# Interleaving the high and low parts of W_out in a channel-attention and feed-forward kernel

## The chip, the cores and the metric

The kernel runs on one NeuronCore of one Trainium2 chip. The metric is the device time of one execution in microseconds (us). A profile of one execution, taken by the hardware profiler, comes with it.

## The reference

For each of four batches, 6080 tokens with 256 channels: q and k are normalised over the tokens, a 256 x 256 attention matrix over the channels is formed, and v is multiplied with it. A feed-forward layer with a leaky ReLU follows.

```python
def _attn_ref(q, k, v, tau):
    qn = q / (np.linalg.norm(q, axis=1, keepdims=True) + 1e-06)
    kn = k / (np.linalg.norm(k, axis=1, keepdims=True) + 1e-06)
    s = kn.transpose(0, 2, 1) @ qn / tau
    a = softmax(s, axis=-1)          # written out in the reference, with 1e-9 in the sum
    return (v @ a).astype(np.float32)

def _moe_ref(x, w_in, w_out):        # w_in 256 x 2048, w_out 2048 x 256, both float64
    h = x @ w_in
    g = np.maximum(0.01 * h, h)
    return (g @ w_out).astype(np.float32)
```

The inputs q, k and v are float32, the two weights are float64, and the result is float32.

## The kernel before, in words

**Number format.** A float32 value is held as two parts in the type float32r: the high part is the value cast to float32r, and the low part is what the cast left out. A product of two such values takes three matmuls: high x high, low x high, high x low. Nearly all products are made so. Only the scores of batch 0 and of the first groups of batch 1 are computed directly from float32 operands.

**Weights.** The float64 weights arrive as pairs of 32-bit words. `f64_load` brings a block of 512 columns into the tile f64_raw (f_raw in the profile), whose last dimension is the pair, and `f64_split` makes the high and low parts: VectorE and ScalarE instructions at lines 323 to 335 rebuild the float32 value, reading the low and high words with a step of two. Then line 338 (ScalarE cast) writes the high part and line 339 (VectorE subtract) the low part. There are 16 such blocks, 8 of W_in and 8 of W_out. `wo_block` gives the destination for W_out: slices of `wo[0]` (high) and `wo[1]` (low). Both are views of the tile `wo_hl` (w_out_split in the profile), which stays in SBUF for the whole kernel. The 8 blocks of W_out are converted in the first 172 us, between other work.

**Tiles.** The tokens are worked on in tiles of 2 x 512 columns, the last of a batch in 2 x 480. There are 6 tiles in each of 4 batches, and 8 pairs of feed-forward blocks in each tile: 192 iterations of the main loop.

**The main loop.** In each iteration `block_product` (line 551) computes the four quarters of the hidden layer with seven block products, three matmuls each. Its stationary operands are the tile w_split, its moving ones v_split. ScalarE and VectorE then take the sums out of PSUM, apply the leaky ReLU (line 562) and split the result into g_split (lines 563 and 565). `ffn_out` (line 597) multiplies g_split with W_out: for each of four quarters and two halves of the output channels three matmuls, so 24 for an iteration, 4608 in all. Their stationary operand is a 128 x 128 piece of `wo[x]`, their moving one a part of g_split with 512 or 480 columns, and they accumulate in four PSUM banks (ps_o).

**Order.** The order on TensorE is written out by hand. `ffn_out` is a generator, and `out(n)` draws its next n matmuls; they stand between the block products of the following iteration, in runs of 5, 5, 8 and the rest, where they fill the time in which ScalarE and VectorE work on the hidden layer. The queues `todo`, emptied by `slot`, put the work for the next batch (casts, scores at line 182, the new weights at line 401) into the gaps. DMAs are issued from the sync engine's queue.

**Each matmul has a weight load of its own**: TensorE loads the stationary operand (LDWEIGHTS, in the profile's row PEld) and then streams the moving operand past it (MATMUL, row PE). The load of one matmul is issued while the one before it is still streaming.

Of the kernel before, what the change touches and what calls it, by code (L numbers as in the profile page):

```python
# [10 lines left out]
F32R = mybir.dt.float32r  # L11
# [6 lines left out]
P = 128  # L18
# [13 lines left out]
def channel_attention_ffn(  # L32
# [18 lines left out]
    B, N, C = q.shape  # L51
    CH = C // P
    DFF = w_in.shape[1]
    NF = DFF // P
# [12 lines left out]
    const = ctx.enter_context(tc.tile_pool(name="const", bufs=1))  # L67
# [6 lines left out]
    def bank(tag, bufs=1):  # L74
        return psum.tile([P, TW], F32, name="ps_" + tag, tag=tag, bufs=bufs)
# [11 lines left out]
    rtau = const.tile([P, 1], F32, name="rtau")  # L87


    wo_hl = const.tile([P, 2 * NF * C + P], F32R, name="w_out_split")  # L90
    wo = [wo_hl[:, x:x + NF * C].rearrange("p (f d) -> p f d", d=C) for x in (0, NF * C + P)]
    zeros = const.tile([P, P], F32, name="zeros")
    nc.vector.memset(zeros, 0.0)

# [759 lines left out]
    for i in range(NTILES):  # L854
        for p in range(NPAIR):
# [6 lines left out]
            x, y, z = bank("x"), bank("y"), bank("z")  # L862
# [63 lines left out]
```

## Time and profile before

| what | value |
|---|---|
| time, median of 2 runs | 2225.53 us (2225.09 to 2225.98) |
| span of the profiled execution, first to last instruction | 2225.9 us |
| mean granted TensorE clock in it | 0.990 |
| TensorE matmuls | 2174.0 us busy, 9940 matmuls |
| weight loads | 1814.1 us busy, 9940 loads |
| VectorE / ScalarE | 1488.5 / 1483.2 us busy |
| matmuls of line 597 (W_out) | 3840 with 512 columns, 768 with 480 |

The profile gives, beside these, the span in 40 slices (busy tenths of each engine, and the clock granted to TensorE in tenths of full speed), the chain of work that ended last, groups of equal instructions with their mean duration, windows with the busy time of each engine, and a timeline. In a timeline row stand the start, the length, the engine, the line, the operation, the output and the inputs, the shape and the count of like instructions that follow one another; a bracket gives idle time ahead of them. Matmuls overlap on TensorE and their ends are modelled, so what a matmul costs is read from the distance between the starts of successive ones.

### The profile page before, as it was taken

Reading aid. Unit: us, or ns where it says so; the run is one execution under the profiler, and the core shown is the slowest. Engines: PE = TensorE matmul, PEld = TensorE weight load, DVE = VectorE, ACT = ScalarE, POOL = GpSimd, SP = SyncE. Lnnn points to the kernel's source line nnn. Section 1 sums busy time; section 2 is a strip of 40 time slices with the busy share of each in tenths; the row PEclk is TensorE's granted clock in tenths of the full one; section 3 lists DMA queues with packets and bytes.
Section 4 is the critical chain, followed back from the end, with each engine's and each line's share of the span. In section 5 each row is a group of like instructions: output and inputs, shape, how many; then the busy total and the mean of one; then the engine's idle time right before and its main releaser. Section 6 shows DMA issues by size and latency. Waiting matters only on the chain.

```text
span 2225.9 us, 27253 instructions
## 1 busy us (share of the span) xinstructions
PE 2174.0 (98%) x9940; PEld 1814.1 (81%) x9940; DVE 1488.5 (67%) x2651; ACT 1483.2 (67%) x2563; POOL 2.8 (0%) x10
## 2 busy tenths in 40 slices
PE   9679999999999999999999999999999999999999
PEld 7467888888888888888887888888888888888887
DVE  7986667666766776666766667676677655556554
ACT  6556777766657777776656777777665666666665
POOL 0000000000000000000000000000000000000000
PEclk9889999999999999999999999999999999999999
DMA  9435343342753434433464344343354432332331
GB/s 347 145 142 200 121 155 134 130 157 83 241 204 112 156 123 145 154 116 138 147 227 156 119 159 159 115 155 129 121 192 156 146 137 83 138 121 100 119 118 36
DMA packets 98967, 324.74 MB, mean 146 GB/s; under 512 B 10257, under 2 KB 22033, under 8 KB 98833
## 3 DMA queue, kind: packets, MB, share of 16 engines
q1 hardware_dynamic: 98832, 323.00, 42.1%
q8 instruction: 78, 1.28, 0.2%
q14 instruction: 57, 0.46, 0.1%
HBM read 264.50 MB, written 58.46 MB: 145 GB/s over the span
## 4 chain that ended last, share of the span: by engine, by line
PE 89%; DVE 5%; DMA 3%; ACT 2%; issue 0%; SPq 0%; ACTq 0%; DVEq 0%
PE ps_o L597 44%; PE ps_x L551 22%; PE ps_z L551 11%; PE ps_y L551 5%; PE ps_s L182 5%; PE ps_s L401 1%; DMA qk_raw<-in_k_dram 1%; DVE h L572 1%; DVE g_split L565 1%; DMA w_dram<-w_rest 1%; ACT h L562 1%; ACT g_split L563 1%; DMA f_raw<-in_w_out_dram 1%; DMA qk_raw<-in_q_dram 1%; DVE v_split L516 0%
## 5 line engine op out<-in xcount | busy, mean ns | idle before, releaser
L597 PE MATMUL ps_o<-g_split,w_out_split 128*128 128x512 f32 (+1 forms) x4608 | 1165.5, 388 | 0.0
L597 PEld LDWEIGHTS ps_o<-g_split,w_out_split 128*128 128x128 f32 x4608 | 867.7, 188 | 175.5
L565 DVE TENSOR_TENSOR g_split<-h,g_split 128x512 fp32r<-128x512 f32 (+1 forms) x768 | 525.0, 684 | 395.3 <-ACT g_split L563 394.4
L551 PE MATMUL ps_x<-v_split,w_split 128*128 128x512 f32 (+1 forms) x2304 | 653.7, 392 | 29.4 <-DVE w_split L439 16.2
L562 ACT ACTIVATE h<-h 128x512 f32<-128x512 f32 (+1 forms) x576 | 361.8, 628 | 292.3 <-DVE h L572 292.3
L578 ACT COPY h<-ps_x 128x512 f32<-128x512 f32 (+1 forms) x576 | 334.3, 580 | 312.4 <-PE ps_x L551 311.7
L551 PEld LDWEIGHTS ps_x<-v_split,w_split 128*128 128x128 f32 x2304 | 423.7, 189 | 114.0 <-ACT h L578 12.4
L563 ACT CAST g_split<-h 128x512 fp32r<-128x512 f32 (+1 forms) x768 | 473.4, 616 | 23.9
L572 DVE TENSOR_TENSOR h<-ps_z,h 128x512 f32<-128x512 f32 (+1 forms) x384 | 262.0, 682 | 284.7 <-ACT h L578 278.0
L551 PE MATMUL ps_z<-v_split,w_split 128*128 128x512 f32 (+1 forms) x1152 | 324.4, 390 | 6.3 <-DVE h L572 6.3
L551 PEld LDWEIGHTS ps_z<-v_split,w_split 128*128 128x128 f32 x1152 | 216.5, 188 | 52.5 <-DVE h L572 8.1
L551 PE MATMUL ps_y<-v_split,w_split 128*128 128x512 f32 (+1 forms) x576 | 162.9, 391 | 0.6 <-ACT w_a L411 0.6
L572 DVE TENSOR_TENSOR h<-ps_y,h 128x512 f32<-128x512 f32 (+1 forms) x192 | 131.3, 684 | 0.6
L551 PEld LDWEIGHTS ps_y<-v_split,w_split 128*128 128x128 f32 x576 | 109.0, 190 | 23.5 <-ACT w_a L411 1.1
L182 PEld LDWEIGHTS ps_s<-qk_split 128*128 128x128 f32 x804 | 114.1, 190 | 11.3 <-issue 1.0
L562 ACT ACTIVATE h<-ps_x 128x512 f32<-128x512 f32 (+1 forms) x192 | 112.8, 587 | 10.8 <-PE ps_x L551 10.8
L182 PE MATMUL ps_s<-qk_split 128*128 128x256 f32 x804 | 118.1, 283 | 0.0
L160 ACT CAST qk_split<-qk_raw 128x512 fp32r<-128x512 f32 x134 | 82.9, 619 | 31.8 <-PE ps_s L182 24.0
L516 DVE TENSOR_TENSOR v_split<-v_raw,v_split 128x512 fp32r<-128x512 f32 (+1 forms) x144 | 98.7, 686 | 4.7
L155 DVE TENSOR_TENSOR sq_acc<-sq_acc,sq 128x512 f32<-128x512 f32 x141 | 96.2, 683 | 0.0
L164 DVE TENSOR_TENSOR qk_split<-qk_raw,qk_split 128x512 fp32r<-128x512 f32 x134 | 91.6, 684 | 2.3 <-ACT qk_split L160 2.3
L152 ACT ACTIVATE sq<-qk_raw 128x512 f32<-128x512 f32 x141 | 88.8, 633 | 2.0 <-DMA qk_raw<-in_k_dram 2.0
(101 smaller groups left out, 726.7 us busy)
## 6 DMA issues: line engine op xcount, KB each, us to landing
w_split<-w_dram SPq DMA_DIRECT2D x184, 896.0 KB, 4.7
qk_raw<-in_q_dram SPq DMA_DIRECT2D x92, 256.0 KB, 3.6
qk_raw<-in_k_dram SPq DMA_DIRECT2D x92, 256.0 KB, 3.8
v_raw<-in_vT_dram SPq DMA_DIRECT2D x40, 512.0 KB, 4.9
out_dram<-o_sb SPq DMA_DIRECT2D x80, 256.0 KB, 4.2
win<-win_dram SPq DMA_DIRECT2D x24, 512.0 KB, 4.1
w_dram<-w_rest SPq DMA_DIRECT2D x24, 512.0 KB, 3.1
w_dram<-w_first SPq DMA_DIRECT2D x24, 384.0 KB, 3.4
```

What stands on the lines that cost most here:

```text
L152: return nc.scalar.activation(out=out, in_=self.chunk(j), func=AF.Square)
L155: return nc.vector.tensor_tensor(out=self.acc[0], in0=self.acc[0], in1=sq, op=ALU.add)
L164: return nc.vector.tensor_tensor(out=sp[:, :, 1, :], in0=self.chunk(j), in1=f32(sp[:, :, 0, :]), op=ALU.subtract)
L182: mm = nc.tensor.matmul(out=s, lhsT=lhsT, rhs=rhs, start=False, stop=last and n == len(passes) - 1, skip_group_check=True,)
L516: last = nc.vector.tensor_tensor(out=sp[:, 1, 0:w], in0=src, in1=f32(sp[:, 0, 0:w]), op=ALU.subtract)
L551: mm = nc.tensor.matmul(out=ps[:, 0:n], lhsT=w[:, x, a, :], rhs=sp[:, y, 0:n], start=first and k == 0, stop=k == 2, skip_group_check=True,)
L562: nc.scalar.activation(out=out[:, 0:n], in_=h[:, 0:n], func=AF.Prelu, alpha=0.01)
L563: issued["act"] = nc.scalar.copy(out=sp[:, 0, 0:n], in_=out[:, 0:n])
L565: issued["dve"] = nc.vector.tensor_tensor(out=sp[:, 1, 0:n], in0=out[:, 0:n], in1=f32(sp[:, 0, 0:n]), op=ALU.subtract)
L572: issued["dve"] = nc.vector.tensor_tensor(out=h[:, 0:n], in0=ps[:, 0:n], in1=h[:, 0:n], op=ALU.add)
L578: issued["act"] = nc.scalar.copy(out=h[:, 0:n], in_=ps[:, 0:n])
L597: issued["pe"] = nc.tensor.matmul(out=o_ps[i][j][h][:, 0:n], lhsT=wo[x][:, f, h * P:(h + 1) * P], rhs=sp[:, y, 0:n], start=p == 0 and earl ...
```

## The change

The tile w_out_split held the 4096 values of the high part of each partition, a gap of 128 values, and the 4096 of the low part. Now it holds pairs: the high and the low part of one value stand side by side, with 64 unused pairs at the end. The tile has 8320 values per partition in both kernels. Every view `wo[x]` now has a step of two values in its last dimension: `f64_split` writes it with that step, and the weight loads of line 597 read their 128 columns with it. Nothing else in the source is changed.

```diff
-    wo_hl = const.tile([P, 2 * NF * C + P], F32R, name="w_out_split")
-    wo = [wo_hl[:, x:x + NF * C].rearrange("p (f d) -> p f d", d=C) for x in (0, NF * C + P)]
+    wo_hl = const.tile([P, NF * C + P // 2, 2], F32R, name="w_out_split")
+    wo = [wo_hl[:, 0:NF * C, x].rearrange("p (f d) -> p f d", d=C) for x in range(2)]
```

## The prediction

> **What bounds the kernel now.** The reading goes from the page's busy shares and slices to its chain, and from there to the weight loads. The first fence holds the page's engine line, the slices of TensorE (PE) and of its granted clock, and the chain of work that ended last.
>
> ```profile
> PE 2174.0 (98%) x9940; PEld 1814.1 (81%) x9940; DVE 1488.5 (67%) x2651; ACT 1483.2 (67%) x2563; POOL 2.8 (0%) x10
> PE   9679999999999999999999999999999999999999
> PEclk9889999999999999999999999999999999999999
> PE 89%; DVE 5%; DMA 3%; ACT 2%; issue 0%; SPq 0%; ACTq 0%; DVEq 0%
> ```
>
> TensorE carries 89% of the chain, and after the third slice it neither rests nor loses clock. The next fence has two tables of windows (busy time and count of each engine, granted clock, DMA share, GB/s). The first two rows are of all instructions: a stretch at half clock, a steady one at full clock. The last two are of the instructions that touch w_out_split alone.
>
> ```profile
> 85.00:89.00 4.00, 3.32 (x9) 2.62 (x9) 2.84 (x8) 1.77 (x3) 0.00 (x0) 0.50 0.41 166
> 300.00:400.00 100.00, 100.00 (x482) 84.26 (x481) 68.60 (x111) 74.63 (x130) 0.00 (x0) 1.00 0.43 150
> ...
> 0.00:172.00 172.00, 28.99 (x106) 21.43 (x106) 5.48 (x8) 4.93 (x8) 0.89 0.59 211
> 172.00:2226.00 2054.00, 1136.56 (x4502) 846.24 (x4502) 0.00 (x0) 0.00 (x0) 1.00 0.41 140
> ```
>
> In 300 to 400 us TensorE is busy all the time, and the two vector engines have 31 and 25 us to spare. 4502 of the 4608 matmuls that use W_out lie behind 172 us, in such stretches. So the question is what paces one matmul after another. A matmul's own duration doesn't tell it, because matmuls overlap; the distance from start to start does. The rows below are of the timeline (start, length, engine, line, tile, count); the first is the fp32 score product of batch 0, the next three are at the half clock, the next four at full clock, and the last is the tail.
>
> ```profile
> 19.68 28.65 PE L182 MATMUL ps_o<-qk_raw 128*128 128x256 f32 x132
> ...
> 86.71 1.48 PE L551 MATMUL ps_z<-v_split,w_split 128*128 128x512 f32 x3
> 87.99 1.48 PE L551 MATMUL ps_x<-v_split,w_split 128*128 128x512 f32 x3
> 89.27 0.63 PE L401 MATMUL ps_y<-win_early,aT 128*128 128x512 f32 x1
> ...
> 1316.30 0.84 PE L551 MATMUL ps_y<-v_split,w_split 128*128 128x512 f32 x3
> 1316.98 1.30 PE L597 MATMUL ps_o<-g_split,w_out_split 128*128 128x512 f32 x5
> 1318.12 0.88 PE L182 MATMUL ps_s<-qk_split 128*128 128x256 f32 x6
> 1318.83 0.40 PE L551 MATMUL ps_x<-v_split,w_split 128*128 128x512 f32 x1
> ...
> 2214.89 6.66 PE L597 MATMUL ps_o<-g_split,w_out_split 128*128 128x480 f32 x30
> ```
>
> At half clock, three fp32r matmuls of 512 columns take 89.27 - 87.99 = 1.28 us, or 426.7 ns each. Halved, that is what 512 columns cost at full clock if nothing else costs: 213.3 ns, 0.417 ns a column. Measured at full clock: (1316.98 - 1316.30) / 3 = 226.7 ns, and five W_out matmuls take 1.14 us, 228 ns each, the same within the rounding. So each fp32r matmul of 512 columns pays 226.7 - 213.3 = 13.4 ns beyond its columns. In the tail 29 steps (6.66 us less the last matmul's own 0.38, from the group rows below) make 216.6 ns for 480 columns that should take 200.0: 16.6 ns beyond. In the fp32 row 131 steps take (28.65 - 0.39) / 131 = 215.7 ns for 256 columns. That is 0.84 ns a column, twice the fp32r one; against two times 256 column times, 213.3 ns, only 2.4 ns are beyond, though a weight load stands before each of those matmuls as well.
>
> The excess is therefore no fixed price of a load and a matmul. It appears where the moving operand is streamed at a column every 0.417 ns, and it all but vanishes where a column takes twice that. I read it as the load's reads of the buffer getting in the way of a stream that has no slack.
>
> The weight loads come next: groups by form (busy, mean ns), and two timeline rows for their pace.
>
> ```profile
> L597 PE MATMUL ps_o<-g_split,w_out_split 128*128 128x512 f32 x3840 | 977.3, 390 | 0.0
> L597 PEld LDWEIGHTS ps_o<-g_split,w_out_split 128*128 128x128 f32 x4608 | 867.7, 188 | 175.5
> L597 PE MATMUL ps_o<-g_split,w_out_split 128*128 128x480 f32 x768 | 188.2, 381 | 0.0
> L182 PE MATMUL ps_o<-qk_raw 128*128 128x256 f32 x192 | 42.8, 386 | 0.0
> L182 PEld LDWEIGHTS ps_s<-qk_raw 128*128 128x128 f32 x40 | 7.4, 190 | 3.9 <-DMA qk_raw<-in_k_dram 2.5 <-issue 0.5
> ...
> 52.87 1.08 PEld L200 LDWEIGHTS ps_y<-ones,sq_acc 128*128 128x128 f32 x8
> 53.87 0.30 PEld L182 LDWEIGHTS ps_s<-qk_raw 128*128 128x128 f32 x2
> ```
>
> A load's record of 188 ns is latency and reading together. Where eight loads follow one another with matmuls of a single column between, they take 53.87 - 52.87 = 1.00 us, at most 125 ns each. So a contiguous load of 128 elements holds its path for up to 125 ns, under a matmul of 213.3 ns: it has some 88 ns of cover. Loads of fp32 and fp32r show the same record (190 and 188 ns), so the two kinds of matmul differ in the stream, not in the load.
>
> **The change part by part.** The matmuls, their order, the DMAs and the queues stay as they are; no wait and no instruction is added. Two things change: how 16 instructions write W_out's parts, and how 4608 loads read them.
>
> The writes. In the conversions, the operand f_raw already holds pairs of words read with a step of two, so the trace prices steps on the vector engines:
>
> ```profile
> L323 DVE TENSOR_SCALAR f_scale<-f_raw 128x512 int32<-128x512 int32 x16 | 6.7, 422 | 1.0 <-DMA f_raw<-in_w_out_dram 1.0
> L515 DVE CAST v_split<-v_raw 128x512 fp32r<-128x512 f32 x120 | 50.1, 419 | 0.0
> L329 ACT ACTIVATE f_raw<-f_raw 128x512 f32<-128x512 uint32 x16 | 10.9, 681 | 13.5 <-DMA f_raw<-in_w_out_dram 10.3 <-DMA f_raw<-in_w_in_dram 3.1
> L338 ACT CAST w_out_split<-f_x 128x512 fp32r<-128x512 f32 x8 | 4.9, 618 | 6.9 <-DVE f_x L335 6.9
> L339 DVE TENSOR_TENSOR w_out_split<-f_x,w_out_split 128x512 fp32r<-128x512 f32 x8 | 5.5, 685 | 0.1
> ```
>
> VectorE reads with a step of two at 422 ns against 419 dense: nothing. ScalarE at line 329 reads and writes with the step, in place, at 681 ns; the dense cast at line 338 takes 618. Eight casts could thus grow by 8 x 63 ns = 0.5 us. A stepped write of VectorE is in no row; its bounds are nothing and a doubling, 8 x 685 ns = 5.5 us. I take 0.5 us for all, nearest to the rows. It falls before 172 us.
>
> The reads. No row shows a stationary operand with a step. Its price per matmul lies between two ends. Below: the whole excess goes, 3840 x 13.4 + 768 x 16.6 = 51.5 + 12.7 = 64 us gained. Above: the stepped load passes over 1024 bytes of a partition instead of 512, and if what it takes from the stream goes with that, the excess doubles: 64 us lost. The value in between depends on which row is the likeness. I take the fp32 row, by a conjecture about pace: a contiguous load moves through the buffer by 4 bytes per 0.98 ns at the slowest (125 ns over 128), which I take as about the pace of an fp32 stream, 4 bytes per 0.84 ns, and half that of the fp32r stream, 4 bytes per 0.417 ns. So load and fp32r stream keep crossing, while beside the fp32 stream, where both go alike, the excess is 2.4 ns. With a step of two the load would move by 8 bytes per 0.84 ns, again level with the fp32r stream. If that row carries over, each matmul keeps 2.4 ns: 512 columns give back 13.4 - 2.4 = 11.0 ns, 480 columns 14.2 ns. Sum: 3840 x 11.0 + 768 x 14.2 = 42.2 + 10.9 = 53.1 us. Of it 4502 / 4608 lies where TensorE is busy throughout: 51.9 us. What could be late next are ScalarE and VectorE, whose spare 25 and 31 us in 100 cover a stretch that shrinks by 2.5.
>
> The Trainium skill speaks against this. "TensorE: Matmul & The Clock Gate", section "Step-by-step: what each phase is for", gives TensorE two independent SBUF read ports and says that loading weights takes no read bandwidth from the running matmul. The trace disagrees as far as 13.4 ns against 2.4 ns need an explanation; by the page the excess would not be the load's doing, and the step's term in the sum would be nothing instead of 51.9 us.
>
> The span becomes 2225.9 - 51.9 + 0.5 = 2174.5 us. The span of the profiled execution (2225.9) stands 0.4 us over the median of the timed runs (2225.53), so no correction is due: rounded to **2175 us**, 2.3% faster.
>
> **The rivals.** *No change of pace.* The load makes 128 reads either way, it has 88 ns of cover, and VectorE's row shows that a step of two costs a reader nothing. If the excess is a cost per load, or per read, every matmul stays at 226.7 ns: 2225.9 + 0.5 = 2226 us. Against it: the excess follows the pace of the stream, so the pattern of reads should matter. The Trainium skill has a rule for this outcome: "SBUF — State Buffer", section "Specifications (TRN2)", asks for at least two hits on a 16-byte line for full bandwidth, which four-byte elements at a step of two still give; the trace agrees on VectorE (422 against 419 ns), and no row shows it for a weight load.
>
> *Slower: the excess doubles.* One mechanism: each piece of the buffer that the load fetches takes a slot from the stream, and the stepped load fetches twice as many. 240 ns for 512 columns, 233 for 480; 64 us, less the 2% before 172 us, make 62.5: 2226 + 62.5 = 2288 us. It decides as soon as twice the fetches no longer fit beside the stream at full clock. For it: the half clock, where there is room, shows no excess at all. Against: the fp32 row has as many fetches a load and hardly any excess.
>
> *Slower still: the load outlasts its cover.* If the step doubled the load itself to 250 ns, it would pace the matmuls from 213.3 ns on: 250 - 226.7 = 23 ns x 3840 + 33 ns x 768 = 115 us, 2341 us; four times as slow, 500 ns each, would be over 1.2 ms more. VectorE's row speaks against any such price. That the change doesn't do what it says is hardly possible: the loads' addresses follow from the tile's layout.
>
> **How the numbers follow.** Excess falls to the fp32 row's: 0.42. No change of pace: 0.33. Doubled excess: 0.19. Load outlasts its cover: 0.06. What a measurement of this kernel can tell from no change is taken as 2%, 44.5 us. The first case passes it unless over 7 of its 51.9 us come back as waits, or part of the excess stays: 0.33 of the 0.42. So faster by over 2% has 0.33; within 2% has 0.09 + 0.33 + 0.01 = 0.43; slower 0.18 + 0.06 = 0.24. The first case's own range is 2162 (whole excess gone) to 2185. Cases of both signs hold much of the chance, so the range reaches from 2162 to the doubled excess, 2290.
>
> **What would show it.** The timeline's W_out matmuls in a steady stretch: about 216 ns from start to start confirms the forecast, 227 the first rival, 240 the second, 250 or more the third; the matmuls of lines 551 and 182 should stay as they are, except beside W_out loads. The casts at lines 338 and 339 should stay under 0.7 us. The chain's share of ps_o L597 should fall. The forecast is wrong if the excess has nothing to do with where the load reads, or if a stepped load is read by another, slower way that no row here shows.

## The result and the profile after

The changed kernel takes 2252.68 us (median of two runs, 2252.03 to 2253.33) against 2225.53 us: slower by a ratio of 1.0122, 95% interval 1.0078 to 1.0165. The forecast was 2175 us. The order of the instructions is the same on every engine.

The page of the changed kernel, its engine line, the slices of TensorE and its clock, and the chain:

```profile
PE 2201.6 (98%) x9940; PEld 1840.5 (82%) x9940; DVE 1493.6 (66%) x2651; ACT 1494.2 (66%) x2563; POOL 2.8 (0%) x10
PE   9689999999999999999999999999999999999999
PEclk9789999999999999999999999999999999999999
PE 92%; DVE 5%; ACT 2%; DMA 1%; issue 0%; SPq 0%; DVEq 0%
```

TensorE is as busy as before, at the same clock. VectorE and ScalarE are busy 5 and 11 us more, with 5% and 2% of the chain as before. So the 27 us must lie in the pace of the matmuls. The timeline of the changed kernel (start, length, count), first at half clock, then in a steady stretch, then with 480 columns and the tail; the last two rows are those of the kernel before, with 480 columns:

```profile
149.46 1.48 PE L551 MATMUL ps_y<-v_split,w_split 128*128 128x512 f32 x3
150.74 1.48 PE L597 MATMUL ps_o<-g_split,w_out_split 128*128 128x512 f32 x3
...
1322.72 2.03 PE L597 MATMUL ps_o<-g_split,w_out_split 128*128 128x512 f32 x8
1324.59 0.85 PE L551 MATMUL ps_x<-v_split,w_split 128*128 128x512 f32 x3
1325.27 0.85 PE L551 MATMUL ps_z<-v_split,w_split 128*128 128x512 f32 x3
...
2236.10 1.89 PE L597 MATMUL ps_o<-g_split,w_out_split 128*128 128x480 f32 x8
2237.83 0.81 PE L551 MATMUL ps_x<-v_split,w_split 128*128 128x480 f32 x3
...
2239.14 6.76 PE L597 MATMUL ps_o<-g_split,w_out_split 128*128 128x480 f32 x30
...
2202.11 1.90 PE L597 MATMUL ps_o<-g_split,w_out_split 128*128 128x480 f32 x8
2203.84 0.81 PE L551 MATMUL ps_x<-v_split,w_split 128*128 128x480 f32 x3
```

Eight W_out matmuls start to start take 1324.59 - 1322.72 = 1.87 us, 233.8 ns each (with an inner step of (2.03 - 0.39) / 7 = 234 ns), where the kernel before had 226.7 to 228. Over all W_out matmuls of 512 columns that start behind 200 us, the means in the two traces are 233.1 and 227.0 ns (from start to start, without gaps over 300 ns, which are waits; so are the means below). So such a matmul now pays about 20 ns beyond its 213.3 ns of columns, not 13.4. The block product behind them stays at 0.68 us for three, 226.7 ns, but over all matmuls of line 551 with 512 columns the mean goes from 227.9 to 228.8 ns: those that stand at a change to or from W_out pay as well.

With 480 columns the step costs next to nothing in the loop: eight matmuls take 1.73 us in both kernels. Only the tail is slower, (6.76 - 0.38) / 29 = 220.0 ns against 216.6, and over all 768 the mean goes from 216.7 to 218.1 ns. At half clock the stepped loads cost nothing: three ps_o matmuls take 1.48 us, as the dense ones of line 551 do. By these means the sum is 3840 x 6.1 = 23 us for W_out at 512 columns, 768 x 1.4 = 1 us at 480, and 3360 x 0.9 = 3 us in line 551: 27 us, as the medians have it. The two profiled spans differ by 24.4 us (2250.3 and 2225.9), as the execution of the kernel before had some 2 us more of waits. The groups by form show the rest:

```profile
L597 PEld LDWEIGHTS ps_o<-g_split,w_out_split 128*128 128x128 f32 x4608 | 893.3, 194 | 170.8
L339 DVE TENSOR_TENSOR w_out_split<-f_x,w_out_split 128x512 fp32r<-128x512 f32 x8 | 5.5, 690 | 0.1
L338 ACT CAST w_out_split<-f_x 128x512 fp32r<-128x512 f32 x8 | 5.3, 667 | 6.8 <-DVE f_x L335 6.8
```

The record of a load grew from 188 to 194 ns. The stepped casts grew from 618 to 667 ns, 0.4 us for eight, and the stepped subtracts from 685 to 690.

### The profile page after: what moved, and what is told of

Its sections match the earlier page's. It is cut to its first block, busy times and chain, and to the rows that moved or that the text cites. A ratio compares the mean times of both kernels' runs of the same rounds, so it can differ in the third digit from the quotient of the medians.

```text
span 2250.3 us, 27253 instructions
## 1 busy us (share of the span) xinstructions
PE 2201.6 (98%) x9940; PEld 1840.5 (82%) x9940; DVE 1493.6 (66%) x2651; ACT 1494.2 (66%) x2563; POOL 2.8 (0%) x10
## 4 chain that ended last, share of the span: by engine, by line
PE 92%; DVE 5%; ACT 2%; DMA 1%; issue 0%; SPq 0%; DVEq 0%
PE ps_o L597 45%; PE ps_x L551 22%; PE ps_z L551 11%; PE ps_y L551 5%; PE ps_s L182 4%; PE ps_o L182 2%; PE ps_s L401 1%; DVE h L572 1%; DVE g_split L565 1%; ACT h L562 1%; DMA w_dram<-w_rest 1%; ACT g_split L563 1%; DMA f_raw<-in_w_out_dram 0%; DVE v_split L516 0%; DVE f_x L334 0%
## 5 line engine op out<-in xcount | busy, mean ns | idle before, releaser
L597 PE MATMUL ps_o<-g_split,w_out_split 128*128 128x512 f32 (+1 forms) x4608 | 1190.5, 393 | 0.0
L597 PEld LDWEIGHTS ps_o<-g_split,w_out_split 128*128 128x128 f32 x4608 | 893.3, 194 | 170.8
```

The lines of the kernel that those rows point to most:

```text
L597: issued["pe"] = nc.tensor.matmul(out=o_ps[i][j][h][:, 0:n], lhsT=wo[x][:, f, h * P:(h + 1) * P], rhs=sp[:, y, 0:n], start=p == 0 and earl ...
```

## The experiments

The prediction's theory was one of pace. Against it stood a fetch theory (a load costs by the pieces it fetches) and a length theory (a stepped load is longer). Later a theory of places was added (what counts is where load and stream start). The expectations call the fetch theory a count theory too, and the theory of places a phase or place theory. Edits are against the changed kernel's two lines unless a whole kernel is new.

**Loads and streams alone.** A new kernel with nothing but runs of 48 matmuls:

```diff
+for i in range(48):
+    nc.tensor.matmul(out=t[:, 0:n], lhsT=w(step)(i), rhs=m(n)(i), start=i == 0, stop=i == 47)
+# w(step): 128 columns of a float32r tile with that step; m(n): n columns of another, in four places in turn
```

> Computes none of the reference: runs of 48 matmuls one after another, each run with another step of the stationary operand, another width or another pattern of the moving operand, on random data already in the buffer. Start to start is read. Fetch theory (each piece of a line that a load fetches takes a slot from a moving stream that has none to spare): fp32r with 512 columns 227 ns dense, 233 at a step of two, and more for each further step, about 247 at a step of four, then flat, since from four on every element is a fetch of its own; the same ns at 480 and 256 columns; next to nothing beside an fp32 stream, at any step. Length theory (a stepped load is only longer, by the 6 ns that its record grew, and the tail of it shows): 227, 233, and then in steps of about 6 ns or a jump once the load outlasts its cover; far more at 256 columns than at 512, and a cost beside fp32 as well. Pace theory of the prediction (level paces don't collide): nothing of the 13 ns left where moving operand and load step alike, so a moving operand with a step of two and a dense load would be worst and the two at equal byte pace best.

Windows over the runs, each from the first start of one run to that of the next, so that a stretch over 48 is the distance from start to start (over 96 for fp32, which takes two matmuls each). In order: 512 columns with a step of 1, 2, 4; dense from element 1; 480 columns with a step of 1, 2; 256 columns with a step of 1, 2, 4; moving operand with a step of 2; load of one repeated element; moving operand one repeated element; fp32 with a step of 1, 2, 4.

```profile
28.09:38.98 10.89, 10.89 (x50) 9.02 (x48) 0.00 (x0) 0.59 (x1) 0.00 (x0) 1.00 0.01 2
38.98:50.18 11.20, 11.20 (x49) 9.30 (x48) 0.00 (x0) 0.59 (x1) 0.00 (x0) 1.00 0.00 0
61.48:72.76 11.28, 11.28 (x49) 11.28 (x49) 0.00 (x0) 0.59 (x1) 0.00 (x0) 1.00 0.00 1
95.82:106.97 11.15, 11.15 (x49) 9.00 (x48) 0.00 (x0) 0.59 (x1) 0.00 (x0) 1.00 0.00 0
129.45:139.84 10.39, 10.39 (x49) 9.00 (x48) 0.00 (x0) 0.59 (x1) 0.00 (x0) 1.00 0.00 0
139.84:150.24 10.40, 10.40 (x49) 9.28 (x48) 0.00 (x0) 0.56 (x1) 0.00 (x0) 1.00 0.00 0
150.24:156.00 5.76, 5.76 (x50) 5.75 (x48) 0.00 (x0) 0.56 (x1) 0.00 (x0) 1.00 0.01 3
156.00:161.76 5.76, 5.76 (x51) 5.76 (x49) 0.00 (x0) 0.38 (x1) 0.00 (x0) 1.00 0.00 0
161.76:172.96 11.20, 11.20 (x51) 11.20 (x49) 0.00 (x0) 0.37 (x1) 0.00 (x0) 1.00 0.01 1
172.96:194.60 21.64, 21.64 (x50) 9.96 (x49) 0.00 (x0) 0.37 (x1) 0.00 (x0) 1.00 0.00 0
216.41:227.41 11.00, 11.00 (x49) 9.04 (x48) 0.00 (x0) 0.59 (x1) 0.00 (x0) 1.00 0.01 1
227.42:237.91 10.49, 10.49 (x50) 9.16 (x48) 0.00 (x0) 0.59 (x1) 0.00 (x0) 1.00 0.00 0
333.29:354.03 20.74, 20.74 (x97) 18.26 (x96) 0.00 (x0) 0.59 (x1) 0.00 (x0) 1.00 0.00 1
354.03:374.75 20.72, 20.72 (x97) 18.87 (x96) 0.00 (x0) 0.37 (x1) 0.00 (x0) 1.00 0.00 0
374.75:396.96 22.21, 22.21 (x97) 22.21 (x97) 0.00 (x0) 0.38 (x1) 0.00 (x0) 1.00 0.00 1
```

The step's price stands alone as in the kernel: 226.9 ns dense, 233.3 at a step of two, and no difference at 480 columns (216.5 and 216.7). Four things follow.

The pace theory falls: a load level with the stream in bytes costs the stream more, not less. With load and stream both at a step of two, which is level again, a matmul takes (216.41 - 194.60) / 48 = 454.4 ns, and beside a dense load (194.60 - 172.96) / 48 = 450.8.

The length theory falls for a step of two: at 256 columns, where a load has only 107 ns of cover, dense and stepped both take 120.0 ns. A step of four does lengthen the load, to 233.3 ns, and the loads then follow one another without a gap (11.20 us of load in 11.20).

What the stream reads matters, as the fetch theory has it: beside fp32 a step of two costs nothing (215.8 ns against 216.0), and where the stream reads one element over and over the excess drops to 218.5 - 213.3 = 5.2 ns.

But the load's fetches don't set the price: a dense load from element 1 fetches one line more than from 0 and takes 232.3 ns, and a load that reads one element over and over, and has the fewest lines to fetch, takes 229.2 ns, more than a dense one. No run streams without loads, so how much of the 13.4 ns beside a dense load is the load's doing was not measured.

The Trainium skill, "SBUF — State Buffer", section "Specifications (TRN2)", asks for at least two hits on a 16-byte line for full bandwidth. For the load by itself these rows agree: 120.0 ns at a step of two, 233.3 at four. For the moving operand they don't: a step of two still gives two hits, and a matmul takes 450.8 ns. "TensorE: Matmul & The Clock Gate", section "Step-by-step: what each phase is for", has it that loads take no read bandwidth from the stream; that the same stream takes 226.9 ns beside one load and 233.3 beside another speaks against that.

**Interleaved, but dense.**

```diff
+    wo_hl = const.tile([P, NF * C // TW, 2, TW], F32R, name="w_out_split")
+    def wo_at(x, at, n):
+        return wo_hl[:, at // TW, x, at % TW:at % TW + n]
```

> High and low parts of W_out are still interleaved, but in blocks of 512 values, so that every load is dense. Step theory: W_out matmuls of 512 columns at 226.7 ns, the time of the kernel before (2226 us, ratio 1.000 within 0.3%). Neighbour theory (it is the addresses, the high part next to the low one, and not the step): 233 ns and some 2252 us.

2222.19 us against 2224.19, ratio 0.999 (0.998 to 0.9999): the price is gone. The neighbour theory falls in this form, with neighbours in blocks of 512; the next kernel tests it for single values.

**Step of two, high and low parts apart.**

```diff
+    wo_hl = const.tile([P, 2, HALF, 2], F32R, name="w_out_split")
+    def wo_at(x, at, n):
+        return wo_hl[:, x, at % HALF:at % HALF + n, at // HALF]
```

> High and low parts lie apart, but in each the first and the second half of the values are interleaved, so that every load has a step of two without the high and low parts side by side. Step theory: 233 ns, 2252 us, ratio 1.012. Neighbour theory: 227 ns and 2226 us.

2252.69 us, ratio 1.0128 (1.0111 to 1.0144). The step carries the whole cost of the change without high and low side by side; which part lies beside which doesn't matter.

**Step of four.**

```diff
+    wo_hl = const.tile([P, PART, 4], F32R, name="w_out_split")
+    def wo_at(x, at, n):
+        return wo_hl[:, at % PART:at % PART + n, 2 * (at // PART) + x]
```

> High and low parts and two halves of the values interleaved, so that loads have a step of four. Fetch theory: the excess grows from 20 ns to 33 ns a matmul of 512 columns, 247 ns from start to start, so 2226 + 4608 x 20 ns = about 2315 us (ratio 1.040). If only half of a line matters (pieces of 8 bytes), nothing more than at a step of two: 233 ns, 2252 us. Pace theory: the load overtakes the stream again and collides more, over 240 ns.

2277.49 us, ratio 1.0238 (1.0223 to 1.0253). No theory had it: over the 2252 us of half a line, far under the 2315 us of counted fetches. The timeline of this kernel, with 512 and with 480 columns:

```profile
1312.33 2.04 PE L597 MATMUL ps_o<-g_split,w_out_split 128*128 128x512 f32 x8
1314.21 0.85 PE L551 MATMUL ps_x<-v_split,w_split 128*128 128x512 f32 x3
...
2209.82 2.06 PE L597 MATMUL ps_o<-g_split,w_out_split 128*128 128x480 f32 x8
2211.72 0.81 PE L551 MATMUL ps_x<-v_split,w_split 128*128 128x480 f32 x3
```

1.88 us for eight, 235 ns, and 1.90 us with 480 columns, 237 ns, where the kernel before took 216. The pace no longer follows the width. The runs alone give the reading: such a load takes 233.3 ns itself, longer than 512 columns, so it is the rival in which the load outlasts its cover, with 233 ns where the prediction put 250.

**Starts and widths alone.** The kernel of the first experiment with runs of 32, the start of load and stream and the number of columns varied ("pair" is a step of two):

> Computes none of the reference: runs of 32 matmuls of fp32r operands as before, with the start of the load, the start of the stream and the number of columns varied. Count theory (a load costs by the number of 16-byte lines it fetches): any dense load that starts on a line costs 227 ns at 512 columns, one that starts inside a line one line more, about 0.2 ns; step of two 233 ns at any start; the difference of 6.7 ns the same for every width. Phase theory (load and stream read on fixed beats, and what counts is how often the two beats fall together): the start of a load inside a line matters by several ns though it adds one line, a load that starts at another place on a line boundary keeps 227 or moves by whole units of 6.7 ns, and the step's price changes with the width, nothing at 480 and 256 columns as already seen, and at others between nothing and 7 ns. If some start gives less than 227 ns, the kernel has a gain to take there.

```profile
25.73 7.42 PE L30 MATMUL ps_dense_at_zero<-mv,wt 128*128 128x512 f32 x32
55.28 7.63 PE L30 MATMUL ps_dense_at_four<-mv,wt 128*128 128x512 f32 x32
77.67 7.62 PE L30 MATMUL ps_dense_at_sixteen<-mv,wt 128*128 128x512 f32 x32
92.56 7.42 PE L30 MATMUL ps_dense_at_sixtyfour<-mv,wt 128*128 128x512 f32 x32
99.81 7.63 PE L30 MATMUL ps_pair_at_zero<-mv,wt 128*128 128x512 f32 x32
137.09 7.52 PE L30 MATMUL ps_pair_at_sixteen<-mv,wt 128*128 128x512 f32 x32
144.45 7.72 PE L30 MATMUL ps_dense_stream_at_one<-mv,wt 128*128 128x512 f32 x32
273.52 5.72 PE L30 MATMUL ps_dense_cols_f<-mv,wt 128*128 128x384 f32 x32
279.07 5.71 PE L30 MATMUL ps_pair_cols_f<-mv,wt 128*128 128x384 f32 x32
```

A run's length less 0.39 us, over 31, is the distance. Dense loads from element 0 and from 64 take 226.8 ns; from 4 or 16, which are whole lines and the same number of fetches, 233.5 and 233.2. Stepped loads lie between 230 and 233.5 at any start. The stream's place matters too: one element late, beside a dense load, makes 236.5 ns. At 384 columns the step costs nothing (5.72 and 5.71 us), and at 504, 496, 488, 464 and 448 columns the same reading gives from 0.6 ns less to 2.9 ns more. So the step's 6.7 ns belong to 512 columns, and there the cheap case is not "dense" but "dense, from the right place"; most other arrangements pay 230 to 236 ns.

**Dense, but one element late**, in the whole kernel:

```diff
+    wo_hl = const.tile([P, 2 * NF * C + P], F32R, name="w_out_split")
+    def wo_at(x, at, n):
+        return wo_hl[:, x * NF * C + OFF + at:x * NF * C + OFF + at + n]   # OFF = 1
```

> Dense loads as in the kernel before, but the high and the low part each start one element, 4 bytes, later in the tile, so that no load begins on a 16-byte line. Phase theory, by the 232.3 ns measured for such loads alone: 3840 x 5.6 ns + what 480 columns add = 22 us, about 2247 us, ratio 1.010, nearly as slow as the step of two. Count theory: 33 lines instead of 32, 2226 to 2227 us, ratio 1.000 to 1.001.

2262.98 us, ratio 1.0168 (1.0155 to 1.0181): slower than the kernel with a step of two above (1.0128), without any step, and 16 us more than expected. The matmuls with 480 columns say where a part of it lies:

```profile
2212.23 2.00 PE L597 MATMUL ps_o<-g_split,w_out_split 128*128 128x480 f32 x8
2214.07 0.82 PE L551 MATMUL ps_x<-v_split,w_split 128*128 128x480 f32 x3
...
2245.45 7.11 PE L597 MATMUL ps_o<-g_split,w_out_split 128*128 128x480 f32 x30
```

Eight in the loop take 1.84 us, 230 ns, against 216 before, and the tail makes (7.11 - 0.38) / 29 = 232 ns. Over all of them the mean is 226.9 ns, 10 ns over the kernel before, or 8 us for 768. More is in line 551, whose operands have not moved: its mean at 512 columns is 231.6 ns against 227.9, or 12 us for 3360. The expectation left that out.

**Only the low part stepped.**

```diff
+    wo_low = wo_hl[:, NF * C + P:].rearrange("p (n s) -> p n s", s=2)
+    def wo_at(x, at, n):
+        return wo_low[:, at % HALF:at % HALF + n, at // HALF] if x else wo_hl[:, at:at + n]
```

> Only the low part of W_out has a step of two (its two halves interleaved), so one load in three. If each stepped load has its own price: a third of 27 us, 9 us, ratio 1.004. If the price comes from the beat of a run of like loads, so that a lone stepped load among dense ones resets nothing: under 3 us, ratio under 1.002, or more than 14 us if every change of pattern costs a settling of its own.

2239.06 us, ratio 1.0064 (1.0051 to 1.0077), 14.6 us for a third of the loads, where a share of 27 us would be 9. By the interval it is 11 to 17 us. The price doesn't add up load by load.

**Places of load and stream, alone.**

> Computes none of the reference: runs of 32 fp32r matmuls again, now with load and stream each starting at 4-byte element 0 to 256 past a 1-kilobyte boundary, dense and with a step of two, and with dense and stepped loads in turn. Relative-place theory (only the distance between load and stream counts): a dense load and a stream that start at the same element give 227 ns wherever that is, and dense loads at 128 and 192 on a stream at 0 give 227 like the one at 64. Absolute-place theory (each has to start on a boundary of 64 elements): 227 only where both do, 230 to 236 else, also at equal starts. In neither do I expect a place under 226 ns; one that is would be a gain for the kernel. Stepped loads 230 to 234 at any place. Dense and stepped in turn: 230 ns if each load has its own price, over 231 if a change of pattern costs as well, as the kernel with one stepped load in three suggests.

```profile
25.38 7.42 PE L30 MATMUL ps_dense_zero_on_zero<-mv,wt 128*128 128x512 f32 x32
84.14 7.62 PE L30 MATMUL _dense_zero_on_thirtytwo<-mv,wt 128*128 128x512 f32 x32
91.60 7.43 PE L30 MATMUL _dense_zero_on_sixtyfour<-mv,wt 128*128 128x512 f32 x32
128.11 7.77 PE L30 MATMUL ps_dense_one_on_one<-mv,wt 128*128 128x512 f32 x32
135.71 7.55 PE L30 MATMUL ps_dense_four_on_four<-mv,wt 128*128 128x512 f32 x32
143.10 7.46 PE L30 MATMUL dense_sixteen_on_sixteen<-mv,wt 128*128 128x512 f32 x32
150.40 7.46 PE L30 MATMUL e_thirtytwo_on_thirtytwo<-mv,wt 128*128 128x512 f32 x32
172.57 7.63 PE L30 MATMUL ndredtwentyeight_on_zero<-mv,wt 128*128 128x512 f32 x32
244.98 7.63 PE L30 MATMUL ps_dense_pair_in_turn<-mv,wt 128*128 128x512 f32 x32
252.45 7.55 PE L30 MATMUL ps_dense_dense_pair<-mv,wt 128*128 128x512 f32 x32
```

A load from 16 on a stream from 16 takes 228.1 ns over its run and one from 32 on 32 the same (both come down to 227 ns in the second half of the run), against 233.2 ns for 16 on 0 (above) and 0 on 32. So the distance between the two counts, in units of 64 elements or 256 bytes. It isn't all: four on four makes 231.0 ns and one on one 238.1, the most in this kernel. The starts count from the start of each tile, and as the source lays them out both tiles start 128 bytes past a multiple of 256, so it is not a boundary of the partition that helps. A stepped load (the eighth row is one, 128 on 0) pays 233.5 at a distance at which a dense one pays 227. Dense and stepped in turn cost as much as all stepped, 233.5 ns, and one in three still 231.0, 4.2 ns over dense: 3840 of those are 16 us, near the low-part kernel's 14.6. At 512 columns no place gave less than the kernel's own.

**Dense, 64 bytes late**, as the kernel one element late, with OFF = 16:

> W_out dense as before, but both parts start 16 elements (64 bytes, four whole lines) later in the tile, so that each load fetches exactly as many lines as before. Place theory: 233.3 ns a matmul of 512 columns like the step of two, so 3840 x 6.7 = 26 us and a little at 480 columns, about 2251 us, ratio 1.011 to 1.015. Count theory: no change, 2224 us.

2255.83 us, ratio 1.0148 (1.0133 to 1.0163): no step, the same lines to fetch, and the cost of the change within the intervals.

**Dense, 256 bytes late**, OFF = 64:

> The same with 64 elements, 256 bytes. Place theory: 226.7 ns, 2224 us, ratio 1.000 within 0.3%; it also shows that moving the parts, and the gap between them, costs nothing by itself. Count theory: the same.

2224.11 us against 2224.31, ratio 1.000 (0.999 to 1.001). As the source of the kernel before lays out its tiles, w_out_split starts at byte 17632 of a partition and the five g_split buffers at 129248 and every 4096 bytes behind; by these places each dense W_out load starts a multiple of 256 bytes from its stream, and 64 elements keep that.

## Why the prediction was wrong, point by point

*What bounds the kernel* held: start to start of the matmuls, with an excess over the columns that only a stream at full pace pays. The excess depends on the stream: none at half clock with stepped loads either, 2.5 ns beside fp32 at a step of two as well, 5.2 ns beside a stream that stays in place. It depends on the load too, by place and step. That the load's reads take slots from the stream, as the prediction read it, is not shown: a load of one repeated element lowers nothing.

*The step that failed* is the choice of the row for the stepped load's price. I took the fp32 row by a conjecture about equal pace, which counted 0.98 and 0.84 ns for 4 bytes as one pace; hence 2.4 ns, and measured were 20 ns. The fp32 row is cheap at a step of one and of two alike (216.0 and 215.8 ns), so its low price goes with its slow stream and says nothing of a load at the stream's pace. The term of 51.9 us gained became 27 us lost: the sign was wrong, and the forecast with it. The range held the time only because it reached to the doubled excess, and 0.43, the largest chance, was on a change within 2%, where the measured 1.2% lies: both are luck, as far as the mechanism goes. The 2% itself was too wide: the last comparison above, of 10 runs with 13, tells 0.1% (0.999 to 1.001). The upper end of the first case's own range, 2185 us, is worked out nowhere.

*The bounds* held: the excess neither vanished nor doubled; at 512 columns it grew by half, and at 480 hardly.

*The cover* held: a load with a step of two fits into 120 ns, under the 213.3 ns of a 512-column stream, so the rival of an outlasted load needed a step of four to appear.

*The rival of a doubled excess* had the direction, with 62.5 us against 27, and not for its reason. Its count of fetches is refuted by the kernel that starts 64 bytes late and loses as much without one fetch more.

*The rival of no change* relied on the load's cover and on VectorE's step at no cost. Both are true (VectorE's stepped subtract takes 690 ns against 685), and neither decides: the load isn't late, and the matmul beside it is slower all the same.

*The writes* were sized right: 0.4 us of the 0.5. The chain's share of line 597, which was to fall, rose from 44% to 45%.

The cause shown is thus: it is the step of the weight loads that costs the 27 us. Dense loads take the cost away and stepped loads without neighbours keep it. The dense W_out loads, at multiples of 256 bytes from their streams, were in the cheapest arrangement found, 13.4 ns a matmul; a step of two pays what most others pay, about 20. What in the buffer makes 256 bytes the unit, how much of the 13.4 ns is the load's doing, why matmuls of line 551 with unmoved operands slow down beside others, and why the step costs nothing at 256, 384 and 480 columns by themselves, stays open.

## What to carry to other kernels

Where TensorE is the bound, read the distance between matmul starts against columns x 0.417 ns; in these fp32r matmuls with a load each, the rest of 13 to 20 ns answered to where and at what step the operands lie, and not to how long a load takes until the load outlasts the stream. Keep stationary pieces of such a kernel dense and at multiples of 256 bytes from the moving operand's start: a stray offset of 4 or 64 bytes cost this kernel 1.5 to 1.7% with no change in the work. A price seen beside one kind of stream should not be carried to another kind; a run of 48 matmuls by itself would have told it.

## What the runs showed of the hardware that I had not expected

- The starting place of a dense load matters by up to 6.7 ns a 512-column matmul, by its distance from the stream's start modulo 256 bytes (226.8 against 233.2 to 233.5 ns); starts 4 or 16 bytes into the tile for both make 238.1 and 231.0 ns all the same.
- The two distances found most often at 512 columns, 226.7 and 233.3 ns, differ by 16 columns' time, 6.7 ns.
- A load that reads one element over and over costs its matmul 229.2 ns, more than a dense load at 226.9.
- A moving operand with a step of two elements halves the stream: 21.64 us / 48 = 450.8 ns a matmul of 512 columns.
- A load with a step of four takes 233.3 ns (11.20 us / 48 at 256 columns), longer than a whole 512-column stream; with a step of two it still fits into 120 ns.
